# The second MLP's output product turned round: weights held, 512 tokens streamed

## The chip, the core and the metric

The kernel runs on one core of a Trainium2 chip. The metric is the time of one launch in microseconds on the device; three runs of the kernel before are shown, and their median counts. Lower is better.

## What is computed

A gated linear attention is followed by two MLPs over 3072 tokens (4 batches of 768), each 384 wide inside and out with a hidden layer of 2048.

```python
# attention: q, k, v, f_logit of shape (4, 8, 768, 48), fp32
f = 1 / (1 + exp(-f_logit))
for t in range(768):
    state = f[t][:, None] * state + outer(k[t], v[t])     # per batch and head
    y[t] = q[t] @ state
x = y.transpose(0, 2, 1, 3).reshape(3072, 384)            # rows: batch, then token

h = x @ w_in;  x = (max(h, 0) + alpha * min(h, 0)) @ w_out    # first MLP
h = x @ w2_in; out = (h - tanh(h)) @ w2_out                   # second MLP, out: (3072, 384) fp32
```

The weights come in as float64 and are decoded on the chip.

## The kernel before

**Precision.** Each product of the MLPs is made of three matmuls: both operands are split into a high part (fp32r) and a rest (fp32r), named wih and wil, woh and wol, xh and xl, gh and gl, and high x high, high x rest and rest x high are summed in PSUM.

**Units and slots.** The MLPs work in 12 units of UT = 512 tokens, u = 0 to 5 for the first MLP and 6 to 11 for the second. Unit c of an MLP takes chunk c of 128 tokens (tokens 128c to 128c + 127) from each of the four batches. A unit has 16 slots, one for each 128 rows of the hidden layer (fc); slots are numbered through, 0 to 95 for the first MLP, 96 to 191 for the second. In slot s, `mlp_in(s)` (lines 383 to 406) makes h, 128 hidden rows by 512 tokens, by nine matmuls with weights as the stationary operand (lines 394 to 396), and g from it (ScalarE and VectorE; in the second MLP tanh on line 406 and h - tanh on line 407). `mlp_out(s - 2)` then adds the output product of two slots earlier to the unit's accumulators, and `mlp_split(s)` makes gh on ScalarE (line 415) and gl on VectorE (line 416).

**The two forms of the output product** (line 438). In the first MLP the weights are stationary: 3 accumulators of 128 output features by 512 tokens, 3 x 3 matmuls of 512 columns a slot. In the second, g is stationary: 4 accumulators of 128 tokens by 384 features, 4 x 3 matmuls of 384 columns. Both stream 4608 columns a slot.

**PSUM.** Eight banks: acc0 to acc2 (one each), "h" (two), "att" (three, for the attention and, in the second MLP, for the fourth accumulator).

**End of a unit.** The accumulators are copied to the tile o in turn by ScalarE and VectorE (lines 447 and 449). In the first MLP one DMA writes o to x1d in DRAM (line 454), which `load_x1` reads back for the second MLP (line 375) and splits into xh and xl. In the second MLP two DMAs of 384 KB write a unit's rows of out (line 452); the last unit writes each of its four accumulators by a DMA of its own. All DMAs are issued by SP's queue, in order. The tile o, the x1 that is read back and the raw weights share two buffers (tag "raw"). The x tiles have two buffers, so the x of a unit can be split as soon as the unit two earlier has made its last h.

**The order.** Attention steps, weight loads and conversions, and loads of x1 are entered in a list with due slots (`put`) and called between the parts of the slots; a scheduler then sets the order on each engine by simulated readiness. The second MLP's weights are loaded from slot 81 on and converted (`convert`, lines 49 to 60 and 199 to 200) every 1.5 slots from slot 86 on, in the buffers that the first MLP's weights leave; `load_x1(c)` for c from 1 on is due in slot 8 of the second MLP's unit c - 1.

Of the kernel before, what the change touches and what calls it, by code (L numbers as in the profile page):

```python
# [10 lines left out]
F32 = mybir.dt.float32  # L11
# [7 lines left out]
B, H, S, D = 4, 8, 768, 48  # L19
NT, DM, DFF = B * S, H * D, 2048  # L20
C = 128
NC = S // C
UT = B * C
# [40 lines left out]
def tile_main(tc, q, k, v, f_logit, w1_in, w1_out, alpha, w2_in, w2_out, out, flag):  # L64
    nc = tc.nc
    with ExitStack() as ctx:
# [9 lines left out]
        ps = ctx.enter_context(tc.tile_pool(name="ps", bufs=1, space=PSUM))  # L76
        ps2 = ctx.enter_context(tc.tile_pool(name="ps2", bufs=2, space=PSUM))
        ps3 = ctx.enter_context(tc.tile_pool(name="ps3", bufs=3, space=PSUM))
# [3 lines left out]
        x1d = dram.tile([128, 3, NT], F32, name="x1d")  # L82
# [7 lines left out]
            out=causal, in_=causal, compare_op=ALU.is_ge, fill=0.0,  # L90
# [11 lines left out]
        for b in range(B):  # L102
            state.append(const.tile([128, NP, D], F32, name=f"state{b}"))
            t = const.tile([128, NP, 2, HW], F32, name=f"blocks{b}")
# [11 lines left out]
        for nm, idle in (("f", 30.0), ("k", 0.0), ("q", 0.0)):  # L116
            padded[nm] = []
            for j in range(NV):
                t = const.tile([128, H, HW], F32, name=f"{nm}{j}")
# [263 lines left out]
        gg, gsplit, acc = {}, {}, {}  # L383
# [35 lines left out]
        def mlp_out(s):  # L419
            m, c, fc = slots[s]  # L420
            n, u = UT, m * NC + c
            gh, gl = gsplit.pop(s)
            wh, wl = w_sb[m, fc // 2, 1]
            r = fc % 2
            first, final = fc == 0, fc == FC - 1
            if first:
                shape = [128, n] if m == 0 else [128, DM]
                acc[u] = [ps.tile(shape, F32, tag=f"acc{j}", name=f"acc{j}") for j in range(3)]
                if m:
                    acc[u].append(ps3.tile(shape, F32, tag="att", name="acc3"))  # L430
            for j, t in enumerate(acc[u]):
                e = slice(j * 128, j * 128 + 128)
                if m == 0:
                    terms = ((wh[:, r, e], gh), (wh[:, r, e], gl), (wl[:, r, e], gh))
                else:
                    terms = ((gh[:, e], wh[:, r]), (gh[:, e], wl[:, r]), (gl[:, e], wh[:, r]))
                for i, (a, b) in enumerate(terms):
                    nc.tensor.matmul(out=t, lhsT=a, rhs=b, start=first and i == 0, stop=final and i == 2)  # L438
            if not final:
                return  # L440
            done = acc.pop(u)
            e = stg.tile([128, len(done), 1536 // len(done)], F32, tag="raw", name="o")
            rows = out.rearrange("(b s) e -> s b e", s=S)[c * C:c * C + C]
            each = 1 if u == 2 * NC - 1 else 2
            for j, t in enumerate(done):
                if j % 2:
                    nc.vector.tensor_copy(out=e[:, j, 0:t.shape[1]], in_=t)
                else:
                    nc.scalar.copy(out=e[:, j, 0:t.shape[1]], in_=t)
                if m == 1 and (j + 1) % each == 0:  # L450
                    js = slice(j + 1 - each, j + 1)
                    nc.sync.dma_start(out=rows[:, js, :], in_=e[:, js, :])
            if m == 0:
                nc.sync.dma_start(out=x1d[:, :, c * UT:c * UT + UT], in_=e)


        ring = ["att", "att", "att", "acc0", "acc1", "acc2", "h", "h"]
# [56 lines left out]
        for i in range(B, NC * B):  # L514
            c, b = divmod(i, B)
# [19 lines left out]
        done = 0  # L535
        for s in range(len(slots) + LAG):
            if s < len(slots):
                mlp_in(s)
            while done < len(work) and work[done][0] < s + 0.5:
                work[done][2](*work[done][3])  # L540
                done += 1
            if s >= LAG:
                mlp_out(s - LAG)
            if s < len(slots):
                mlp_split(s)
            while done < len(work) and work[done][0] < s + 1:
                work[done][2](*work[done][3])
                done += 1
# [152 lines left out]
```

## Time and profile before

| | us |
|---|---|
| median of three runs | 987.1 |
| lowest and highest | 986.56, 987.81 |
| the profiled execution, its time | 987.65 |
| its span | 985.8 |
| TensorE busy | 947.8 |
| VectorE busy | 556.9 |
| ScalarE busy | 407.5 |

PE is TensorE's matmuls, PEld its weight loads, DVE VectorE, ACT ScalarE, SP the queue that issues the DMAs. A matmul's recorded duration overlaps with the next one, so TensorE's pace is read from start to start. The span has three stretches: attention with the first MLP (to about 500 us), the rest of the first MLP with the conversion of the second MLP's weights (to about 583), and the second MLP.

### The profile page before, as it was taken

To read this page: it belongs to the slowest core of one execution; us is meant where nothing else is said; L and a number is where in the kernel's file an instruction comes from. 1 tells how busy PE (TensorE), PEld (TensorE's weight loads), DVE (VectorE), ACT (ScalarE), POOL (GpSimd) and SP (SyncE) were. 2 spreads that over 40 slices of the span, in tenths; PEclk is the share of its full clock that TensorE was granted. 3 is DMA by queue.
4 is the path that set the end of the run, shared out by engine and by line. 5 is a ranking of instruction groups with operands and counts; after the bars stand their busy time and mean duration, and the time that the engine had idled before them with its cause. 6 is when DMAs were issued, how large, how long until landed. Compare 5 with 4: busy or idle time off the path is not lost.

```text
span 985.8 us, 13474 instructions
## 1 busy us (share of the span) xinstructions
PE 947.8 (96%) x5395; PEld 807.0 (82%) x5395; DVE 556.9 (56%) x902; ACT 407.5 (41%) x723; POOL 11.9 (1%) x35
## 2 busy tenths in 40 slices
PE   4779899999999999999999999999999999999997
PEld 3668667888888878888888889999999999999996
DVE  5889998655654655566348989443343433433332
ACT  2446464444434444443356655332332322322322
POOL 2100000000000000000000000000000000000000
PEclk9879999999999999999999999999999999999999
DMA  9985752311331142220014444120010100000001
GB/s 145 195 142 128 140 144 41 87 29 37 73 57 25 33 89 41 41 73 9 9 37 157 143 137 137 33 64 1 1 64 1 43 23 1 33 1 1 33 1 35
DMA packets 124230, 61.12 MB, mean 62 GB/s; under 512 B 104304, under 2 KB 109312, under 8 KB 124160
## 3 DMA queue, kind: packets, MB, share of 16 engines
q1 hardware_dynamic: 124160, 60.19, 27.4%
q8 instruction: 44, 0.72, 0.3%
q14 instruction: 26, 0.21, 0.1%
HBM read 48.77 MB, written 9.44 MB: 59 GB/s over the span
## 4 chain that ended last, share of the span: by engine, by line
PE 85%; DVE 6%; DMA 4%; SPq 2%; ACT 1%; issue 1%; DVEq 0%; ACTq 0%
PE acc L438 38%; PE h L394 13%; PE h L395 13%; PE h L396 13%; DMA raw<-in_moe_w_in_dram 3%; PE y L310 2%; PE sc L263 2%; PE y L286 2%; PE kt L213 1%; DVE dec L58 1%; PE ft L213 1%; DMA raw<-in_moe_w_out_dram 1%; DVE down L231 1%; SPq L153 1%; PE m L345 1%
## 5 line engine op out<-in xcount | busy, mean ns | idle before, releaser
L394 PE MATMUL h<-x,wih 128*128 128x512 f32 x576 | 229.4, 398 | 2.6 <-ACT x L303 2.3
L396 PE MATMUL h<-x,wil 128*128 128x512 f32 x576 | 227.2, 395 | 0.0
L395 PE MATMUL h<-x,wih 128*128 128x512 f32 x576 | 227.2, 394 | 0.0
L416 DVE TENSOR_TENSOR gl<-g,gh 128x512 fp32r<-128x512 f32 x192 | 132.3, 689 | 83.2 <-PE acc L438 46.7
L415 ACT CAST gh<-g 128x512 fp32r<-128x512 f32 x192 | 119.1, 620 | 113.1 <-DVE g L407 62.4
L407 DVE TENSOR_TENSOR g<-h,g 128x512 f32<-128x512 f32 x96 | 66.4, 691 | 172.1 <-ACT g L406 172.0
L406 ACT ACTIVATE g<-h 128x512 f32<-128x512 f32 x96 | 57.4, 598 | 188.2 <-PE h L396 188.2
L402 DVE SCALAR_TENSOR_TENSOR g<-neg,alpha_neg,g 128x512 f32<-128x512 f32 x96 | 71.9, 749 | 101.8 <-ACT neg L401 101.0
L438 PE MATMUL acc<-woh,gh 128*128 128x384 f32 x384 | 129.3, 337 | 0.0
L438 PE MATMUL acc<-wol,gh 128*128 128x384 f32 x384 | 129.1, 336 | 0.0
L438 PE MATMUL acc<-woh,gl 128*128 128x384 f32 x384 | 128.0, 337 | 0.0
L394 PEld LDWEIGHTS h<-x,wih 128*128 128x128 f32 x576 | 108.9, 189 | 23.1 <-ACT x L303 2.7
L396 PEld LDWEIGHTS h<-x,wil 128*128 128x128 f32 x576 | 108.6, 189 | 23.2
L395 PEld LDWEIGHTS h<-x,wih 128*128 128x128 f32 x576 | 108.9, 189 | 19.4 <-DVE x L304 0.3
L438 PE MATMUL acc<-gl,woh 128*128 128x512 f32 x288 | 113.4, 394 | 1.1 <-DVE gl L416 0.9
L438 PE MATMUL acc<-gh,wol 128*128 128x512 f32 x288 | 112.9, 392 | 0.0
L438 PE MATMUL acc<-gh,woh 128*128 128x512 f32 x288 | 108.3, 402 | 3.7 <-ACT gh L415 3.5
L400 ACT ACTIVATE g<-h 128x512 f32<-128x512 f32 x96 | 57.4, 598 | 118.8 <-PE h L396 117.8
L438 PEld LDWEIGHTS acc<-woh,gh 128*128 128x128 f32 x384 | 72.2, 188 | 4.5
L438 PEld LDWEIGHTS acc<-wol,gh 128*128 128x128 f32 x384 | 72.1, 188 | 4.3
L438 PEld LDWEIGHTS acc<-woh,gl 128*128 128x128 f32 x384 | 71.9, 188 | 0.0
L438 PEld LDWEIGHTS acc<-gh,woh 128*128 128x128 f32 x288 | 53.5, 188 | 15.4 <-ACT gh L415 4.8
(90 smaller groups left out, 937.7 us busy)
## 6 DMA issues: line engine op xcount, KB each, us to landing
raw<-in_moe_w_out_dram SPq DMA_DIRECT2D x16, 768.0 KB, 4.4
raw<-in_moe_w_in_dram SPq DMA_DIRECT2D x8, 768.0 KB, 4.6
f<-in_f_logit_dram SPq DMA_DIRECT2D x24, 192.0 KB, 2.8
k<-in_k_dram SPq DMA_DIRECT2D x24, 192.0 KB, 3.2
q<-in_q_dram SPq DMA_DIRECT2D x24, 192.0 KB, 3.7
raw<-in_moe_w_in_dram SPq DMA_DIRECT2D x16, 288.0 KB, 5.2
x1d<-o SPq DMA_DIRECT2D x6, 768.0 KB, 4.3
x1raw<-x1d SPq DMA_DIRECT2D x6, 768.0 KB, 4.9
```

What stands on the lines that cost most here:

```text
L213: nc.tensor.transpose(t[:, p], a[:, 2 * p:2 * p + 2, :].rearrange("t h d -> t (h d)"), ident)
L263: nc.tensor.matmul(out=sc[h][:, p], lhsT=s["kd"][r, p], rhs=s["qd"][r, p], start=True, stop=True)
L394: nc.tensor.matmul(out=h, lhsT=a, rhs=xh[:, r], start=(r == 0), stop=False)
L395: nc.tensor.matmul(out=h, lhsT=a, rhs=xl[:, r], start=False, stop=False)
L396: nc.tensor.matmul(out=h, lhsT=b, rhs=xh[:, r], start=False, stop=(r == 2))
L400: nc.scalar.activation(out=g, in_=h, func=ACTF.Relu)
L402: nc.vector.scalar_tensor_tensor(out=g, in0=neg, scalar=alpha_neg[:, fc:fc + 1], in1=g, op0=ALU.mult, op1=ALU.add)
L406: nc.scalar.activation(out=g, in_=h, func=ACTF.Tanh)
L407: nc.vector.tensor_tensor(out=g, in0=h, in1=g, op=ALU.subtract)
L415: nc.scalar.copy(out=gh, in_=g)
L416: nc.vector.tensor_tensor(out=gl, in0=g, in1=gh.bitcast(F32), op=ALU.subtract)
L438: nc.tensor.matmul(out=t, lhsT=a, rhs=b, start=first and i == 0, stop=final and i == 2)
```

## The change

Units 6 to 10 get the first MLP's form of the output product: weights stationary, 512 tokens streamed, three accumulators of 128 features by 512 tokens. Units 6, 8 and 10 keep them in the three "att" banks, units 7 and 9 in acc0 to acc2. At such a unit's end VectorE transposes each accumulator in blocks of 32x32 from PSUM to o, and 12 DMAs (one for each accumulator and group of 32 partitions, 64 KB in runs of 128 bytes) write the blocks to their rows of out. Unit 11 keeps g stationary, four accumulators and its four DMAs.

A unit of the second MLP is now 512 successive tokens in the order of out, not a chunk from each batch. For this the first MLP's units write x1d in the order batch, token: four DMAs of 192 KB in runs of 512 bytes in place of one of 768 KB in runs of 2 KB. The read of x1d stays one DMA of 768 KB.

```diff
--- before.py
+++ after.py
@@ -424,13 +424,17 @@
             r = fc % 2
             first, final = fc == 0, fc == FC - 1
             if first:
-                shape = [128, n] if m == 0 else [128, DM]
-                acc[u] = [ps.tile(shape, F32, tag=f"acc{j}", name=f"acc{j}") for j in range(3)]
-                if m:
+
+                shape = [128, DM] if u == 2 * NC - 1 else [128, n]
+                if u >= NC and u % 2 == 0:
+                    acc[u] = [ps3.tile(shape, F32, tag="att", name=f"acc{j}") for j in range(3)]
+                else:
+                    acc[u] = [ps.tile(shape, F32, tag=f"acc{j}", name=f"acc{j}") for j in range(3)]
+                if u == 2 * NC - 1:
                     acc[u].append(ps3.tile(shape, F32, tag="att", name="acc3"))
             for j, t in enumerate(acc[u]):
                 e = slice(j * 128, j * 128 + 128)
-                if m == 0:
+                if u < 2 * NC - 1:
                     terms = ((wh[:, r, e], gh), (wh[:, r, e], gl), (wl[:, r, e], gh))
                 else:
                     terms = ((gh[:, e], wh[:, r]), (gh[:, e], wl[:, r]), (gl[:, e], wh[:, r]))
@@ -440,18 +444,29 @@
                 return
             done = acc.pop(u)
             e = stg.tile([128, len(done), 1536 // len(done)], F32, tag="raw", name="o")
-            rows = out.rearrange("(b s) e -> s b e", s=S)[c * C:c * C + C]
-            each = 1 if u == 2 * NC - 1 else 2
+            if m and u < 2 * NC - 1:
+
+                rows = out[c * UT:c * UT + UT].rearrange("(k t) (j i f) -> j i t k f", t=32, j=3, i=4)
+                for j, t in enumerate(done):
+                    nc.vector.transpose(out=e[:, j], in_=t)
+                    for i in range(4):
+                        nc.sync.dma_start(
+                            out=rows[j, i], in_=e[32 * i:32 * i + 32, j].rearrange("t (k f) -> t k f", f=32)
+                        )
+                return
             for j, t in enumerate(done):
                 if j % 2:
                     nc.vector.tensor_copy(out=e[:, j, 0:t.shape[1]], in_=t)
                 else:
                     nc.scalar.copy(out=e[:, j, 0:t.shape[1]], in_=t)
-                if m == 1 and (j + 1) % each == 0:
-                    js = slice(j + 1 - each, j + 1)
-                    nc.sync.dma_start(out=rows[:, js, :], in_=e[:, js, :])
+                if m:
+                    r0 = c * UT + j * 128
+                    nc.sync.dma_start(out=out[r0:r0 + 128], in_=e[:, j])
             if m == 0:
-                nc.sync.dma_start(out=x1d[:, :, c * UT:c * UT + UT], in_=e)
+                for b in range(B):
+                    nc.sync.dma_start(
+                        out=x1d[:, :, b * S + c * C:b * S + c * C + C], in_=e[:, :, b * C:b * C + C]
+                    )
 
 
         ring = ["att", "att", "att", "acc0", "acc1", "acc2", "h", "h"]
```

## Rows read from the trace of the kernel before

**Rows 1.** The page: TensorE's busy time, its granted clock by slices, the chain.
```profile
PE 947.8 (96%) x5395; PEld 807.0 (82%) x5395; DVE 556.9 (56%) x902; ACT 407.5 (41%) x723; POOL 11.9 (1%) x35
...
PEclk9879999999999999999999999999999999999999
...
PE 85%; DVE 6%; DMA 4%; SPq 2%; ACT 1%; issue 1%; DVEq 0%; ACTq 0%
```

**Rows 2.** The page's costliest groups: matmuls, with idle time ahead of them.
```profile
L394 PE MATMUL h<-x,wih 128*128 128x512 f32 x576 | 229.4, 398 | 2.6 <-ACT x L303 2.3
...
L438 PE MATMUL acc<-woh,gh 128*128 128x384 f32 x384 | 129.3, 337 | 0.0
...
L438 PE MATMUL acc<-gh,woh 128*128 128x512 f32 x288 | 108.3, 402 | 3.7 <-ACT gh L415 3.5
```

**Rows 3.** Timeline of TensorE, second MLP: start us, us, engine, line, operation.
```profile
702.25 0.39 PE L394 MATMUL h<-x,wih 128*128 128x512 f32 x1
...
704.33 0.33 PE L438 MATMUL acc<-woh,gh 128*128 128x384 f32 x1
...
706.43 0.39 PE L394 MATMUL h<-x,wih 128*128 128x512 f32 x1
...
970.19 0.39 PE L394 MATMUL h<-x,wih 128*128 128x512 f32 x1
```

**Rows 4.** Windows: stretch and its length, busy us by engine, granted clock, DMA.
```profile
702.24:970.18 267.94, 267.94 (x1345) 242.82 (x1345) 97.71 (x145) 85.60 (x146) 0.00 (x0) 1.00 0.06 18
```

**Rows 5.** Timeline of TensorE, first MLP after the attention's last step.
```profile
523.74 0.39 PE L394 MATMUL h<-x,wih 128*128 128x512 f32 x1
...
531.90 0.39 PE L394 MATMUL h<-x,wih 128*128 128x512 f32 x1
```

**Rows 6.** Timeline: around the first 384-column matmul, and at the end.
```profile
577.39 0.69 DVE L407 TENSOR_TENSOR g<-h,g 128x512 f32<-128x512 f32 x1
...
580.86 0.39 PE L394 MATMUL h<-x,wih 128*128 128x512 f32 x1
...
582.90 0.33 PE L438 MATMUL acc<-woh,gh 128*128 128x384 f32 x1
...
973.34 0.33 PE L438 MATMUL acc<-woh,gh 128*128 128x384 f32 x1
...
977.67 0.33 PE L438 MATMUL acc<-wol,gh 128*128 128x384 f32 x1
```

**Rows 7.** Groups of VectorE by line and shape.
```profile
L447 DVE COPY o<-acc 128x512 f32<-128x512 f32 x6 | 4.1, 684 | 0.2 <-PE acc L438 0.2
...
L447 DVE COPY o<-acc 128x384 f32<-128x384 f32 x12 | 6.5, 553 | 4.4 <-PE acc L438 4.4
...
L231 DVE TENSOR_TENSOR_SCAN down<-gate,carry 128x516 f32<-128x516 f32 x24 | 29.5, 1229 | 0.0
```

**Rows 8.** Timeline of one slot: g, gl, and the product that needs gl.
```profile
701.03 0.69 DVE L407 TENSOR_TENSOR g<-h,g 128x512 f32<-128x512 f32 x1 [2.12 <-ACT g L406]
...
702.41 0.69 DVE L416 TENSOR_TENSOR gl<-g,gh 128x512 fp32r<-128x512 f32 x1 [0.69 <-PE acc L438]
...
708.51 0.33 PE L438 MATMUL acc<-woh,gh 128*128 128x384 f32 x1
```

**Rows 9.** The page's DMA issues: KB each, median us from issue to landing.
```profile
f<-in_f_logit_dram SPq DMA_DIRECT2D x24, 192.0 KB, 2.8
...
x1d<-o SPq DMA_DIRECT2D x6, 768.0 KB, 4.3
```

**Rows 10.** Waits of SP's DMA queue from 480 to 700 us: total, times, longest.
```profile
SPq L164 <- DMA x1d<-o: 3.2, 1, 3.2
```

**Rows 11.** Timeline of VectorE: the second MLP's last input weights.
```profile
613.87 0.95 DVE L200 TENSOR_TENSOR wil<-dec,wih 128x768 fp32r<-128x768 f32 x1
```

**Rows 12.** Windows of two stretches in which weights are converted.
```profile
540.00:570.00 30.00, 30.00 (x134) 24.82 (x134) 28.56 (x43) 19.83 (x33) 0.00 (x0) 1.00 0.43 132
...
583.00:623.00 40.00, 40.00 (x204) 36.41 (x203) 35.38 (x52) 22.81 (x35) 0.00 (x0) 1.00 0.44 139
```

## The prediction

> **What bounds the kernel now.** [...] Then the costliest groups: the matmuls of the two output products (line 438) and of the input products (lines 394 to 396) were preceded by hardly any idle time, 2.6 and 3.7 us where there was any [rows 2]. So in the second MLP nothing that another engine does is late; only TensorE's own spacing of matmuls counts there. A "mean ns of one" in those groups is no price, since matmuls overlap: the price is the distance from start to start, which the timeline shows.
>
> In the second MLP one slot (9 matmuls of 512 columns into h, 12 of 384 into the accumulators) takes 4.18 us: 2.08 for the h part, 2.10 for the output part [rows 3]. Over 64 slots, from 702.25 to 970.19, it is 267.94 / 64 = 4.1866 us, with 1344 matmuls in that stretch [rows 3, 4]. In the late first MLP, where a slot is 18 matmuls of 512 columns, 36 of them start in 531.90 - 523.74 = 8.16 us: 226.7 ns each, 4.08 us a slot [rows 5]. The first MLP's output product has just the form that the change gives to the second.
>
> Two more stretches split the difference. At the end of the kernel, where only 384-column matmuls are left, 25 of them take 977.67 - 973.34 = 4.33 us: 173.2 ns each. And h matmuls that already belong to the second MLP (the tanh units have begun, line 407), but stand before the first 384-column matmul, take 2.04 / 9 = 226.7 ns [rows 6]. So (226.7 - 173.3) / 128 = 0.417 ns is the price of a column, and 13.3 ns come with every matmul whatever its width. Nine and twelve undisturbed matmuls would need 9 x 226.7 + 12 x 173.3 = 4120 ns; the slot takes 4186.6. The missing 66.6 ns show where the widths alternate: the nine h matmuls take 2.08 us there instead of 2.04, the twelve 2.10 instead of 2.08 [rows 3, 6].
>
> **The change, part by part.** *The output product of units 6 to 10.* 5 units x 16 slots = 80 slots go from 9 + 12 matmuls to 9 + 9, all of 512 columns. The columns stay the same, 12 x 384 = 9 x 512 = 4608. Gone are 3 matmuls' fixed part, 3 x 13.3 = 40 ns, and the 66.6 ns of alternation, since the new slot is in form that of [rows 5]: 4186.6 - 4080 = 106.6 ns. TensorE is the bound through all 80 slots, so 80 x 106.6 = **8.5 us**. The lower bound for this term is the fixed part alone, 80 x 40 = 3.2 us, if the 66.6 ns belonged to the second MLP and not to alternation; I take 8.5 because the h matmuls just ahead of the first 384-column one run at 226.7.
>
> [...] The rows have 226.7 and 173.3 ns [rows 5, 6]. [...]
>
> *Unit 11* keeps 12 matmuls of 384 columns; its 16 slots and the tail stay: nothing.
>
> *Accumulators.* Units 6, 8 and 10 take the three "att" banks, so neighbours no longer share banks. The matmuls of line 438 on 384 columns had no idle time before them [rows 2]; there is nothing to win. For unit 11 the fourth bank is one that unit 10's first transposition frees; it is wanted only behind nine h and nine output matmuls, some 3.6 us after unit 10's end, and TensorE waits there only if that first transposition is not done by then.
>
> *VectorE's transpositions.* Per unit 3 transpositions of 128x512 out of PSUM in place of 2 copies on VectorE and 2 on ScalarE. The trace has none. Nearest rows: the copy 128x512 out of PSUM at 684 ns below, the scan 128x516 at 1229 ns above, VectorE's dearest operation of such a width [rows 7]; I take the copy, also one input in and one output of the same shape. That makes 2.1 to 3.7 us per unit on VectorE. What is queued behind them is gl of the same slot. In the steady slot g ends at 701.03 + 0.69 = 701.72, gl starts at 702.41, and the output product that needs it starts at 708.51 [rows 8], 708.3 with slots of 4.08. With the three transpositions between g and gl, gl ends at 701.72 + 3t + 0.69; that is in time up to t = 1.96 us, beyond both bounds. Cost: nothing, gain excluded, since no matmul waited on the copies.
>
> [...]
>
> *The output's DMAs.* 12 of 64 KB per unit in place of 2, in runs of 128 bytes, 512 a DMA, all on SP's queue. The nearest row is the load of f: 192 KB in runs of 192 bytes, 1024 of them, 2.8 us from issue to landing [rows 9]. Twelve one after the other at that price are 34 us, inside the 65 us of the next unit. Behind them on SP stands the load of a later unit's x1, which has most of a unit's time left. Cost nothing; with 65 / 12 = 5.4 us each it would begin to cost.
>
> *The writes of x1d* become 4 DMAs of 192 KB in place of one of 768 KB, 4.3 us to landing [rows 9]. Behind the last one on SP stand loads of the second MLP's weights, one of which waited 3.2 us for such a write [rows 10]. If the four ran end to end at 4.3 us, the landing would be 13 us later; side by side about nothing. The cover is the slack of the weights: the last input weights are ready at 613.87 + 0.95 = 614.8 [rows 11], and are first used in unit 6's slot 14, twelve slots after h at 580.86, that is at 580.9 + 12 x 4.187 = 631.1 (629.8 with the shorter slots). Slack 15 us: nothing, in either case.
>
> *Units of 512 tokens in order.* The second MLP's unit 0 now needs x1d of the first MLP's units 0 to 3, all written some 16 slots before its turn, the others need all six, and unit 1's turn is 16 slots after the last write. Nothing.
>
> *VectorE while weights are converted.* Slots get shorter while its work stays. From 583 to 623 it is busy 35.4 of 40 us; ten shorter slots make that 35.4 of 38.9, 91%. From 540 to 570 it was busy 28.6 of 30, 95%, and TensorE had no idle time [rows 12]. Cost: nothing, up to 2 us if an order of instructions made for other durations fits worse.
>
> **Sum.** The profiled execution took 987.65 us (span 985.8), 0.55 above the median of the three runs, 987.1. 987.65 - 8.5 = 979.1; against the median 978.6. I predict 978.6.
>
> **The rivals.**
> 1. *Only the fixed part goes.* If the irregular spacing belongs to the second MLP's stage (tanh on ScalarE, x from DRAM) and not to alternating widths, the gain is 3.2 us: 983.9. For it: it is seen in this stage only. Against it: the nine h matmuls at 580.86 [rows 6]. Chance 0.08.
> 2. *Columns alone count.* 4608 columns before and after, so no gain: 987.1. For it: the columns are the greater part of the price. Against it: two stretches of one width each, whose difference leaves 13.3 ns per matmul [rows 5, 6]. Chance 0.04. [...]
> 3. *The transpositions hold gl up: slower.* VectorE takes its queue in order, so from t = 1.96 us each on the output product two slots later waits, by 3t - 5.9 us in each of 5 units. The gain is eaten at 3t - 5.9 = 1.7, t = 2.53 us; at four times the copy's price, t = 2.74, the loss is 5 x 2.3 = 11.5 us and the time 990.1. For it: no transposition is in the trace. Against it: the dearest row of that width is 1.23 us. Chance 0.06.
> 4. *The weight stage gets tight.* Late weights or a VectorE that falls behind while it converts take back up to 2 us: 980.6. For it: 91% busy, and the weight loads stand behind four writes. Against it: 95% without a stall, and 15 us of slack. Chance 0.08.
>
> **How the numbers follow.** The forecast has 0.74. The range takes in the spread of the runs below it (0.5 us, and half a microsecond for the sum) and the first and fourth rival above: 977.6 to 984.0, which leaves out rivals 2 and 3 (0.10) and the edges of the other cases. A measurement of this kernel can tell about 0.2% (2 us) from no change. Faster by more than that: forecast and rivals 1 and 4, 0.90. Within: rival 2, 0.04. Slower: rival 3, 0.06.
>
> **What would show it.** In the changed kernel's timeline the slots of units 6 to 10 should be 18 matmuls in 4.08 us, at 226 or 227 ns each, and those of unit 11 4.187 us as before. The group of 384-column matmuls should shrink from x384 to x64 per term, the 512-column ones grow from x288 to x528. A slot of 4.15 us would mean rival 1; idle time before line 438 that a gl releases, rival 3, with the transposition's duration beside it; idle time before lines 394 to 396 or 438 between 570 and 640 that weights release, rival 4. The forecast is wrong if slots of eighteen 512-column matmuls are not evenly spaced there, or if the idle time of TensorE grows by more than a microsecond or two anywhere.

## The result

The changed kernel takes 977.36 us (median of four runs, 976.37 to 979.25) beside 986.83 (four runs) for the kernel before: ratio 0.9905, 95% interval 0.9888 to 0.9922. The forecast was 978.6, inside that interval, but the measured median lies 0.24 us below the low end of the range, 977.6. Timed again (e1, below) the same kernel gave 979.27 beside 987.72: ratio 0.9913, interval 0.9890 to 0.9936.

The profiled execution took 976.37 us, span 974.7: 11.1 us less span than the one of before. That is more than the 8.5 us of the sum, and where the rest lies is the first question to the trace. The page's part 1 for the changed kernel, and its costliest groups of the output product:

```profile
PE 939.2 (96%) x5155; PEld 773.7 (79%) x5155; DVE 560.3 (57%) x907; ACT 403.5 (41%) x713; POOL 11.4 (1%) x35
...
L442 PE MATMUL acc<-gl,woh 128*128 128x512 f32 x528 | 207.4, 393 | 0.6 <-DVE gl L416 0.4
L442 PE MATMUL acc<-gh,wol 128*128 128x512 f32 x528 | 206.7, 391 | 0.0
L442 PE MATMUL acc<-gh,woh 128*128 128x512 f32 x528 | 200.4, 396 | 3.5 <-ACT gh L415 3.4
```

Beside [rows 1, 2]: 240 matmuls fewer, 528 per term with 512 columns as foreseen (384 columns: 64 per term, not shown), and the idle time ahead of the product is about what it was (3.5 us before its first term, 3.7 before the change). The timeline of TensorE in the second MLP of the changed kernel, the first h matmul of three slots, and the first output matmul of one:

```profile
700.64 0.39 PE L394 MATMUL h<-x,wih 128*128 128x512 f32 x1
...
702.68 0.39 PE L442 MATMUL acc<-gh,woh 128*128 128x512 f32 x1
...
704.72 0.39 PE L394 MATMUL h<-x,wih 128*128 128x512 f32 x1
...
896.48 0.39 PE L394 MATMUL h<-x,wih 128*128 128x512 f32 x1
```

704.72 - 700.64 = 4.08 us a slot, and (896.48 - 700.64) / 48 = 4.080 over 48 slots, where [rows 3] had 4.1866. The h part is 2.04 us now. This is the forecast's slot. Unit 11, which kept the old form, takes 4.187 us a slot as before (10 slots from 917.16 to 959.03 us).

To see where the other 2.6 us went, three landmarks: the first h matmul of slot 20, of slot 96 (the second MLP's first) and of slot 176 (near the end of the units that changed). Before:

```profile
184.42 0.47 PE L394 MATMUL h<-x,wih 128*128 128x512 f32 x1
...
571.34 0.39 PE L394 MATMUL h<-x,wih 128*128 128x512 f32 x1
...
907.39 0.39 PE L394 MATMUL h<-x,wih 128*128 128x512 f32 x1
```

After (slot 176 stands above, at 896.48):

```profile
181.80 0.47 PE L394 MATMUL h<-x,wih 128*128 128x512 f32 x1
...
568.72 0.39 PE L394 MATMUL h<-x,wih 128*128 128x512 f32 x1
```

From slot 20 to 96 both take 386.92 us. From 96 to 176 it is 336.05 before and 327.76 after, 8.29 us less. The last two changed output slots lie behind that: from slot 176 to the start of the last matmul it is 70.97 us before and 70.72 after, 0.25 less. Together that is 8.54 us, the 8.5 of the forecast. But at slot 20 the changed kernel is already 2.62 us ahead, in a stretch in which every engine has the same instructions in the same order in both kernels (two pairs of neighbouring matmuls aside), but for the writes of x1d, the first of which the changed kernel issues at 168.5 us. That is the part to be explained.

### The profile page after: what moved, and what is told of

Its sections match the earlier page's. It is cut to its first block, busy times and chain, and to the rows that moved or that the text cites. A ratio compares the mean times of both kernels' runs of the same rounds, so it can differ in the third digit from the quotient of the medians.

```text
span 974.7 us, 13074 instructions
## 1 busy us (share of the span) xinstructions
PE 939.2 (96%) x5155; PEld 773.7 (79%) x5155; DVE 560.3 (57%) x907; ACT 403.5 (41%) x713; POOL 11.4 (1%) x35
## 4 chain that ended last, share of the span: by engine, by line
PE 84%; DVE 7%; DMA 4%; SPq 2%; ACT 1%; issue 1%; DVEq 0%; ACTq 0%
PE acc L442 38%; PE h L394 13%; PE h L396 12%; PE h L395 12%; DMA raw<-in_moe_w_in_dram 4%; PE sc L263 2%; PE y L310 2%; PE y L286 1%; PE kt L213 1%; DVE down L231 1%; PE ft L213 1%; DVE dec L55 1%; PE m L345 1%; PE qt L213 1%; ACT mag L49 1%
## 5 line engine op out<-in xcount | busy, mean ns | idle before, releaser
L442 PE MATMUL acc<-gl,woh 128*128 128x512 f32 x528 | 207.4, 393 | 0.6 <-DVE gl L416 0.4
L442 PE MATMUL acc<-gh,wol 128*128 128x512 f32 x528 | 206.7, 391 | 0.0
L442 PE MATMUL acc<-gh,woh 128*128 128x512 f32 x528 | 200.4, 396 | 3.5 <-ACT gh L415 3.4
L442 PEld LDWEIGHTS acc<-gh,woh 128*128 128x128 f32 x528 | 98.6, 188 | 24.6 <-ACT gh L415 4.6
L442 PEld LDWEIGHTS acc<-gl,woh 128*128 128x128 f32 x528 | 99.6, 189 | 22.2 <-DVE gl L416 2.2
L442 PEld LDWEIGHTS acc<-gh,wol 128*128 128x128 f32 x528 | 99.5, 189 | 20.5
L401 ACT ACTIVATE neg<-h 128x512 f32<-128x512 f32 x96 | 56.9, 593 | 0.0
L49 ACT ACTIVATE mag<-raw 128x768 f32<-128x768 f32 x32 | 29.0, 905 | 61.1 <-DMA raw<-in_moe_w_in_dram 34.5
L263 PEld LDWEIGHTS sc<-qd,kd 48*128 48x128 f32 x384 | 24.1, 193 | 9.0 <-issue 5.2
L55 DVE SCALAR_TENSOR_TENSOR dec<-raw,dec 128x768 int32<-128x768 int32 x32 | 31.0, 969 | 0.1
```

What stands on the lines that cost most here:

```text
L263: nc.tensor.matmul(out=sc[h][:, p], lhsT=s["kd"][r, p], rhs=s["qd"][r, p], start=True, stop=True)
L401: nc.scalar.activation(out=neg, in_=h, func=ACTF.Relu, scale=-1.0)
```

## The experiments

**e1: the changed kernel again.** No edit.

> The changed kernel, unaltered, timed again. Two theories on the 0.9 us by which the result beat the forecast. Theory A (spacing): the change is worth 80 slots x 106.6 ns = 8.5 us and nothing else; the rest is the spread of the opening, in which both kernels issue the same instructions in the same order but the changed kernel's profiled execution happened to be 2.6 us ahead at 160 us. Then the ratio is 0.9914 (978.3 beside 986.8), within 0.001. Theory B (opening): the change itself makes the opening shorter. Then the ratio is 0.9904 or lower, down to 0.9887 (2.6 us more), and the profile is again some 2.6 us ahead at slot 20.

Ratio 0.9913, interval 0.9890 to 0.9936. That is theory A's ratio, but the interval takes in theory B's 0.9904 as well; the landmarks in the timeline decide:

```profile
184.36 0.47 PE L394 MATMUL h<-x,wih 128*128 128x512 f32 x1
...
571.28 0.39 PE L394 MATMUL h<-x,wih 128*128 128x512 f32 x1
...
899.03 0.39 PE L394 MATMUL h<-x,wih 128*128 128x512 f32 x1
```

The same program that was 2.62 us ahead at slot 20 is now 0.06 ahead; from 96 to 176 it takes 327.75, as in the first execution, and from slot 20 to the end of the span 792.96 us, where the first execution took 792.86. So theory A: what differs lies ahead of slot 20. Over the twelve profiled executions of this study slot 20 began between 181.46 us (e5) and 185.17 (e7), two executions on the same chip, and slot 96 386.9 to 387.5 us later. So the opening differs by up to 3.7 us from one execution to the next.

A part of this can be read from the two first traces: the first h matmul of slots 0, 2 and 16. Before:

```profile
58.17 0.80 PE L394 MATMUL h<-x,wih 128*128 128x512 f32 x1 [2.33 <-ACT x L303]
...
65.21 0.40 PE L394 MATMUL h<-x,wih 128*128 128x512 f32 x1
...
159.42 0.48 PE L394 MATMUL h<-x,wih 128*128 128x512 f32 x1
```

After:

```profile
56.68 0.50 PE L394 MATMUL h<-x,wih 128*128 128x512 f32 x1 [1.05 <-ACT x L303]
...
61.26 0.39 PE L394 MATMUL h<-x,wih 128*128 128x512 f32 x1
...
156.80 0.48 PE L394 MATMUL h<-x,wih 128*128 128x512 f32 x1
```

The lead is 1.49 us at slot 0, 3.95 at slot 2 and 2.62 at slot 16, some 12 us before the first write of x1d is issued: no instruction that the change touches has run by then. The same 18 matmuls of slots 0 and 1 took 7.04 us in the one trace, at a mean granted clock of 0.58, and 4.58 in the other, at 1.00. An idle time of TensorE of 3.8 us before and 4.4 after ended at 52.5 and 51.9 us; the granted clock was 0.50 from 53.8 to 64.0 us before, and from 52.7 to 56.1 after. So 2.46 us of the difference came with the clock in these two slots. The mean clock does not order the openings, though: up to slot 20 it was 0.94 in both traces, and 0.91 in e1, which stood where before did. What makes the low stretches and their length, and what the first loads of f add (TensorE waits 7.6 us for them before, 6.8 after), was not varied and stays open.

**e2: the order of tokens alone.** Every unit of the second MLP keeps the old product; x1d and out are in the new order.

```diff
-                shape = [128, DM] if u == 2 * NC - 1 else [128, n]
-                if u >= NC and u % 2 == 0:
+                shape = [128, DM] if m else [128, n]
+                if False:
...
-                if u < 2 * NC - 1:
+                if m == 0:
                     terms = ...
...
-            if m and u < 2 * NC - 1:
+            if False:
```

> Only the order of tokens and its DMAs: units of 512 tokens in order, four writes of x1d a unit, every unit of the second MLP with the old output product (12 matmuls of 384 columns, copies, one DMA for each accumulator). Theory A (spacing): the order is worth nothing, ratio 1.000 (986.8), slots of 4.187 us in the second MLP. Theory B (opening, through the writes of x1d): 0.9 to 2.6 us faster, ratio 0.999 to 0.9974.

987.73 us beside 987.72: ratio 0.9998, interval 0.9982 to 1.0015. The order and its four writes cost and bring nothing that this comparison can tell: it excludes the 2.6 us of theory B, not the 0.9. In the profile slot 20 begins at 184.73 us, 0.31 later than before, and from slot 96 to 176 it takes 336.16 us beside 336.05.

**e3: the form alone.** The old order of tokens, one write of x1d a unit, new form in units 6 to 10.

```diff
-                rows = out[c * UT:c * UT + UT].rearrange("(k t) (j i f) -> j i t k f", t=32, j=3, i=4)
+                rows = out.rearrange("(b s) e -> b s e", s=S)[:, c * C:c * C + C].rearrange(
+                    "b (k t) (j i f) -> j i t b k f", t=32, j=3, i=4
+                )
...
+                        for b in range(B):
                             nc.sync.dma_start(out=rows[j, i][:, b], in_=...)
...
-                for b in range(B):
-                    nc.sync.dma_start(out=x1d[:, :, b * S + c * C:b * S + c * C + C], in_=...)
+                nc.sync.dma_start(out=x1d[:, :, c * UT:c * UT + UT], in_=e)
```

> Only the form: units 6 to 10 with weights stationary and 512 tokens streamed, VectorE's transpositions, but units of one 128-token chunk from each batch as before, one write of x1d a unit; the transposed blocks go out in 48 DMAs of 16 KB a unit. Theory A (spacing): the whole gain, ratio 0.9914 (978.3), slots of 4.08 us. Theory B, with the order of tokens as the source of the extra: also 0.9914, while e1 is lower. A cost of the 48 DMAs, if they hold up SP's queue (48 x 0.4 to 0.6 us = 19 to 29 us of issue in the 65 us of a unit), would show as idle TensorE after a unit's end; expected none.

979.37 us, ratio 0.9921, interval 0.9896 to 0.9945, and 327.76 us from slot 96 to 176: the whole gain of the slots is the form's. The 48 DMAs keep SP's queue issuing for 24 us a unit, and no matmul waits for it. The order of tokens has no part in the gain, then; it saves 36 DMAs a unit, at no difference in time that these intervals can tell.

**e4: 448 columns in the old product.** Unit by unit as before, with 64 zeros behind each block of output weights.

```diff
...
-                shape = [128, n] if m == 0 else [128, DM]
+                shape = [128, n] if m == 0 else [128, DM + 64]
...
-                    terms = ((gh[:, e], wh[:, r]), (gh[:, e], wl[:, r]), (gl[:, e], wh[:, r]))
+                    vh, vl = (w[:, p:p + DM + 64] for w in (wh, wl))
+                    terms = ((gh[:, e], vh), (gh[:, e], vl), (gl[:, e], vh))
...
```

> The kernel before, but the second MLP's output product streams 448 columns in place of 384: 64 zeros stand behind each block of output weights, so the result is the same and the twelve matmuls a slot are wider. It asks what makes the 66.6 ns a slot that two widths in turn cost beyond 9 x 226.7 + 12 x 173.3. At 0.417 ns a column 448 columns take 200.0 ns, so an undisturbed slot takes 9 x 226.7 + 12 x 200 = 4440 ns. Theory A1 (any two widths in turn disturb): the slot is longer than 4440 by tens of ns, 4470 to 4510, and the h matmuls are uneven. Theory A2 (a matmul of 173 ns is shorter than the recorded weight load of 188 ns, and the lag is made up in the wider ones): 200 is longer than 188, so the slot is 4440, all h matmuls 226 or 227 ns. Theory C (the second MLP's stage disturbs whatever the widths): the h matmuls take 2.08 us a slot as before. The time is 96 x 0.25 to 0.32 us longer than before's, 1011 to 1018.

1015.58 us, one run. The timeline of TensorE, the last but one slot of the last unit, then the matmuls of 448 columns that stand alone at the end:

```profile
992.14 0.39 PE L399 MATMUL h<-x,wih 128*128 128x512 f32 x1
...
994.20 0.36 PE L446 MATMUL acc<-woh,gh 128*128 128x448 f32 x1
...
996.63 0.39 PE L399 MATMUL h<-x,wih 128*128 128x512 f32 x1
...
998.68 0.36 PE L446 MATMUL acc<-woh,gh 128*128 128x448 f32 x1
...
1004.96 0.37 PE L446 MATMUL acc<-wol,gh 128*128 128x448 f32 x1
```

The slot takes 4.49 us, in theory A1's bounds, but not for A1's reason alone. The 31 matmuls of the end take 6.28 / 31 = 202.6 ns each where nothing alternates: 448 columns have a slower pace of their own than the 200.0 on the line through 384 and 512. With it an undisturbed slot is 9 x 226.7 + 12 x 202.6 = 4471 ns. The 64 slots from 709.51 to 996.63 take 4.486 us each, so two widths in turn cost some 15 to 20 ns here, not 66.6; the h part takes 2.06 us. So the price of the turn is smaller between these two widths, and it does not vanish above the 188 ns of a weight load, as A2 had it. More pairs of widths were not tried.

**e5: 384 columns everywhere in the second MLP.**

```diff
-            n = UT
+            n = UT if m == 0 else 384
             xh, xl = xt[m * NC + c]
+            xh, xl = xh[:, :, 0:n], xl[:, :, 0:n]
...
-                if m:
-                    acc[u].append(ps3.tile(shape, F32, tag="att", name="acc3"))
...
```

> The kernel before, with a part left out: the second MLP takes only 384 of each unit's 512 tokens (three of the four batches), so that its h matmuls and its output matmuls all have 384 columns; the fourth batch is not computed or written, and a slot has 9 + 9 matmuls. Theory A (two widths in turn cost the 66.6 ns): every matmul starts 173.3 ns after the one before and a slot takes 18 x 173.3 = 3120 ns. Theory C (the second MLP's stage, or g as the stationary operand, costs it): the first dozen matmuls of a slot are uneven as before and the slot takes 3120 + 50 to 70. Theory L (384 columns are too few for a weight load recorded at 188 ns, and wide matmuls only let the lag show): 18 x 188 = 3384. The time is 96 x (4.187 - 3.12) = 102 us shorter than before's under A, 885.

882.76 us, one run of a kernel that leaves out the fourth batch, 105 us less than before. Timeline of TensorE, one slot and the start of the next:

```profile
699.80 0.33 PE L395 MATMUL h<-x,wih 128*128 128x384 f32 x1
...
701.36 0.33 PE L437 MATMUL acc<-woh,gh 128*128 128x384 f32 x1
...
702.92 0.33 PE L395 MATMUL h<-x,wih 128*128 128x384 f32 x1
```

3.12 us a slot, 1.56 for nine h and 1.56 for nine output matmuls, 173.3 ns each. The second MLP's stage (tanh, x from DRAM, g as the stationary operand) disturbs nothing when the widths are equal, and 384 columns are not held back by the weight load. Theory A; C and L fall, and with C the forecast's first rival.

**e10: half as many turns.** The kernel before, two slots of the second MLP at a time.

```diff
-        gp = ctx.enter_context(tc.tile_pool(name="gp", bufs=3))
+        gp = ctx.enter_context(tc.tile_pool(name="gp", bufs=4))
...
+            pairs = s >= NC * FC + 2
+            if pairs and s % 2 == 0 and s < len(slots):
+                mlp_in(s)
+                mlp_in(s + 1)
-            if s < len(slots):
+            if not pairs and s < len(slots):
                 mlp_in(s)
```

> The kernel before, old output product in all units, but from the second MLP's third slot on two slots are taken together on TensorE: 18 h matmuls of 512 columns, then 24 output matmuls of 384 (gh and gl have four buffers in place of three). The same matmuls, with half as many changes of width. If the 66.6 ns are the price of one change from 384 to 512 columns and back (theory A, per change), two slots take 18 x 226.7 + 24 x 173.3 + 66.6 = 8307 ns, a slot 4153, and the kernel is 94 x 33 ns = 3.1 us faster than before. If they belong to the matmuls themselves (per matmul), two slots take 8373 ns and the time is that of before.

982.87 us beside 986.88 in the one run each of this comparison. The timeline of TensorE, from the output matmuls of one pair to those of the next:

```profile
700.58 0.33 PE L438 MATMUL acc<-woh,gh 128*128 128x384 f32 x1
...
704.77 0.39 PE L394 MATMUL h<-x,wih 128*128 128x512 f32 x1
...
706.85 0.39 PE L394 MATMUL h<-x,wih 128*128 128x512 f32 x1
...
708.89 0.33 PE L438 MATMUL acc<-woh,gh 128*128 128x384 f32 x1
```

A pair takes 708.89 - 700.58 = 8.31 us, the 8307 ns of theory A per change. The first nine h matmuls after the turn take 2.08 us, the other nine 2.04: the price is paid once per turn, in the first matmuls after it. From slot 96 to 176 this kernel takes 333.83 us, 2.22 less than before, and from there to the last matmul 70.44, 0.53 less: 2.75 of the 3.1 us expected. The single times differ by 4.0 us: 0.9 more is in the tail from the last matmul's start to the end (6.54 us beside 7.47), and openings differ by more than what is left.

**e7 and e11: the transpositions four and eight times.**

```diff
-                    nc.vector.transpose(out=e[:, j], in_=t)
+                    for _ in range(4):        # e11: 8
+                        nc.vector.transpose(out=e[:, j], in_=t)
```

> The changed kernel with every transposition made four times over (nine more on VectorE per unit, same result). It tests the cover that the forecast gave to the transpositions, 3t up to 5.9 us a unit. One takes 0.69 us here and starts 0.62 to 0.65 after the one before, so four stand for t = 2.6. By the forecast's cover 3t - 5.9 = 1.9 us a unit, 9.5 us in five units; by the changed kernel's own trace (gl ends some 4.2 us before its product) 9 x 0.63 - 4.2 = 1.5 us a unit, 7 us. So 7 to 10 us above the changed kernel, about the time before the change, with idle TensorE ahead of the output product and gl as its releaser. If VectorE's queue has more cover than I see, the time is that of the changed kernel.

> The changed kernel with every transposition made eight times (21 more on VectorE per unit, 13 us at 0.62 us each). With four it cost nothing, and there g and gl stood between the transpositions on VectorE. By the forecast's rule (all of a unit's transpositions ahead of gl) it would be 3t - 5.9 = 9 us a unit, 45 us in all. If g and gl are set between them, what counts is VectorE's free time, some 2.7 us a slot, and that a unit's banks are wanted again only a unit later: 13 us find room in five or six slots, and the time is that of the changed kernel, but for unit 11, whose fourth bank waits for unit 10's first accumulator: eight times 0.62 us against 3.6 us of other matmuls, 1 to 3 us of idle TensorE once.

980.78 and 980.08 us, one run each, with no wait of TensorE from 560 us on in either. From slot 96 to 176 they take 327.86 and 327.88 us, 0.1 more than the changed kernel, and from 176 to the last matmul 70.72 and 70.78 where the changed kernel has 70.72. Expected were 7 to 10 us for four, and 1 to 3 for eight. VectorE at the end of unit 6 in the kernel with four:

```profile
646.43 0.72 DVE L452 STREAM_TRANSPOSE o<-acc 128x512 f32<-128x512 f32 x1 [2.00 <-PE acc L442]
647.07 0.65 DVE L407 TENSOR_TENSOR g<-h,g 128x512 f32<-128x512 f32 x1
647.64 2.49 DVE L452 STREAM_TRANSPOSE o<-acc 128x512 f32<-128x512 f32 x4
...
650.06 0.65 DVE L416 TENSOR_TENSOR gl<-g,gh 128x512 fp32r<-128x512 f32 x1
650.63 1.90 DVE L452 STREAM_TRANSPOSE o<-acc 128x512 f32<-128x512 f32 x3
```

The scheduler, which orders the instructions before the kernel runs, sets g and gl between the transpositions. The next unit but one wants their banks, so they spread over VectorE's free time, and gl is late by what stands ahead of it in one slot, not by all of them: its gh was ready at 648.37 us, and it starts at 650.06, after the four of 2.49 us.

**e8 and e9: the last unit in the new form too.** In e8 its 12 DMAs go out on SP's queue, in e9 every second one on ScalarE's.

```diff
-                shape = [128, DM] if u == 2 * NC - 1 else [128, n]
+                shape = [128, n]
...
-            if m and u < 2 * NC - 1:
+            if m:
...                                             # e9 only:
+                        q = nc.scalar if u == 2 * NC - 1 and i % 2 else nc.sync
-                        nc.sync.dma_start(out=rows[j, i], in_=...)
+                        q.dma_start(out=rows[j, i], in_=...)
```

> The changed kernel, with the last unit also in the new form: its 12 DMAs all on SP's queue. Its 16 slots should gain 16 x 106.6 = 1.7 us. Behind the last matmul stand three transpositions and 12 issues at 0.53 us, 6.4 us, in place of two copies on each engine and 4 issues, 2.3 us: the tail grows by 3 to 4 us. Net 1.5 to 2.5 us slower than the changed kernel. If the issues of the first two accumulators are over before the last matmul ends, it is faster by up to 1 us.

> As the run before, with half of the last unit's 12 DMAs issued by ScalarE's queue, which has nothing else to do there. Six issues on each queue, 3.2 us, so the tail is about as long as the changed kernel's, and the 1.7 us of the slots stay: 1 to 1.7 us faster than the changed kernel, ratio to the kernel before about 0.990.

Ratios 0.9922 (0.9895 to 0.9949) and 0.9918 (0.9893 to 0.9943): neither can be told from the changed kernel by its time. The profiles part them. From slot 176 to the last matmul both take 69.13 us where the changed kernel has 70.72, so the slots give 1.6 us; from the last matmul's start to the end of the span e8 has 10.99 and e9 10.02 us, the changed kernel 7.46 (7.57 in e1). The issues of the last unit's output, in e8:

```profile
966.73 7.46 SPq L448 DMA_DIRECT2D out_dram<-o  x12
```

and in e9:

```profile
968.51 5.06 SPq L449 DMA_DIRECT2D out_dram<-o  x6
968.51 5.27 ACTq L449 DMA_DIRECT2D out_dram<-o  x6
```

Twelve issues take 7.5 us on one queue here (6.3 to 6.4 in four of the five units before, 7.3 in the other). On two, six each should have taken half; they take 5.1 to 5.3. The issues were longer: the six on ScalarE's queue took from 0.32 to 1.59 us, with 0.57 in the middle, where the 66 on SP's queue, most of them alone, had 0.50 in the middle. One of 1.6 to 1.7 us stands on each queue, but e8 has such a one too (1.55), with one queue; what makes it was not varied. So e9, expected 1 to 1.7 us faster, is by its one profile some 1 us slower, and e8 1.9, within the 1.5 to 2.5 expected. By these profiles the last unit's old form is worth keeping.

## Why the prediction was right, and where it was not

*The output product.* Right in place, mechanism and size: 4.080 us a slot, 80 x 106.6 ns = 8.5 us, and 8.54 in the traces. That there is a gain settles rival 2. The price of alternating widths holds in e5 (none without alternation) and e10 (66.6 ns per turn, 33 saved per slot when there is one turn for two slots), and with e5 rival 1 falls. The fixed part, 13.3 ns "whatever its width", describes 384 and 512 columns, the widths of the sum; at 448 e4 found 202.6 ns a matmul, not 200.0. In the changed kernel 512 columns take 226.7 ns, 4.08 us / 18, as in [rows 5].

*The step that failed is the range,* in "How the numbers follow": half a microsecond for the spread of the runs and half for the sum. The sum needed none of it; the spread was sized too small. I took it from three runs that lay within 1.25 us; 17 runs of the same kernel beside e1 to e4 lie between 985.66 and 992.89. Medians move with it: that of the kernel before went from 987.1 to 986.83 with a fourth run, which alone is more than the 0.24 us by which the range was missed, and was 987.72 beside e1; that of the changed kernel was 977.36, then 979.27. The first difference of medians beat the sum by 0.94 us (986.83 - 977.36 = 9.47 against 8.53), the second by nothing (987.72 - 979.27 = 8.45).

No run lays that 0.9 us to the change: the landmarks show the form's gain at 8.5 in each execution, and the part that varies lies ahead of slot 20. In the profile the changed kernel's lead was complete before the first instruction that differs. The spread goes with TensorE's clock: of the 17 runs, the four with the longest times had a mean granted clock of 0.981 to 0.985, the four with the shortest 0.988 to 0.992. That is a tendency and not a proof, since only the profiled executions can be taken apart. Whether the median came out inside the range, as in e1, or just below it was luck. Two medians of the changed kernel lie 1.9 us apart; with that for the spread the low end would have been 976.7.

*Accumulators and unit 11.* No wait, as said. That unit 11 would wait if the first transposition were late could not be brought about: with eight of each (e11) 70.78 us from slot 176 on, against 70.72. There the scheduler put only nine of unit 11's first twelve 384-column matmuls behind the first nine h (909.85 to 911.27 us) and the rest behind the next h, so the fourth bank was wanted later. The claim itself stays untested.

*VectorE.* The transposition costs what I took for it, the copy's price; the changed kernel's VectorE groups by form:

```profile
L451 DVE STREAM_TRANSPOSE o<-acc 128x512 f32<-128x512 f32 x15 | 10.0, 695 | 10.0 <-PE acc L442 10.0
...
L459 DVE COPY o<-acc 128x512 f32<-128x512 f32 x6 | 4.1, 684 | 0.2 <-PE acc L442 0.2
```

695 ns against 684. But the third rival's condition was wrong. It put all of a unit's transpositions ahead of gl, with a limit of 1.96 us each; the changed kernel already had g between the first and the second one (642.36, 643.00 and 643.58 us at the end of unit 6), and e7 and e11 show that 2.5 and 5 us for each accumulator do no harm. The verdict (no cost) was right; its threshold was not a property of this kernel, whose scheduler sets the order.

*DMAs.* The twelve of a unit take 6.3 to 6.4 us to issue in four units and 7.8 in one, and land in 2.0 us each in the middle, against the 2.8 that I took from [rows 9]; the last unit's four writes of x1d take 2.57 us to issue, and a write 2.5 to land. From the changed kernel's page:

```profile
x1d<-o SPq DMA_DIRECT2D x24, 192.0 KB, 2.5
```

and from its list of waits on SP's queue, beside [rows 10]:

```profile
SPq L164 <- DMA x1d<-o: 1.7, 3, 0.7
```

The longest wait of a weight load for such a write fell from 3.2 to 0.7 us; the fear of 13 us was far off, in the harmless direction.

*Weights.* TensorE has no wait from 560 us to the end, so the fourth rival did not occur. VectorE was busy 34.95 of 40 us from 583 to 623, 87% and not the 91% that I worked out (34.33, 86%, with the window set 2.62 us earlier, as the execution was), and bore the shorter slots.

## What to carry to other kernels

Where TensorE alone is the bound, price a change of form by start-to-start distances in stretches that already have the new form, and add up the slot: the slot here came out as 4.080 us, as summed, though the count of columns had not changed. Keep matmuls of equal width together where the trace shows a price; two widths in turn cost 66.6 ns per turn here with 384 and 512 columns, so batching slots brings a part of the gain without any change of form (2.75 us by e10's profile). And take the width of the range from how much single runs differ, above all in stretches that the change does not touch, not from three that happen to agree.

## What the runs showed of the hardware that I had not expected

A turn from 384 columns to 512 and back costs 66.6 ns beyond the sum of the two paces (4186.6 a slot against 4120, before; 8.31 us for two slots with one turn, e10), one between 448 and 512 only 15 to 20 (e4). The pace is not a line in the columns: 226.7 ns at 512, 202.6 at 448 (200.0 on the line; e4, one run), 173.3 at 384 (e5). What in TensorE makes either was not found; it is not the 188 ns of a recorded weight load alone, since 384 columns run at 173.3 when nothing alternates (e5).

The granted clock of the opening differs between executions of the same instructions: the 18 matmuls of slots 0 and 1 took 7.04 us at a mean of 0.58 and 4.58 at 1.00 (before, after).

Small-run DMAs issued by two queues at once did not issue twice as fast: 12 of 64 KB in runs of 128 bytes took 6.3 to 7.8 us from one queue and 5.3 from two (after, e8; e9, one execution).
